# Start addresses of rings, pads, mask and unit matrix moved by 64 bytes in a kernel that mixes a Fourier layer with windowed attention

## The chip, the cores and the metric

One core of a Trainium2 chip. The metric is the device time of one execution in microseconds (us); below, "the time" is the median of three timed executions, and "the profiled execution" is one more, taken with the hardware profiler.

## The reference

The input `x` is 2048 rows of 512 floats. Two branches are computed from it and mixed row by row with a gate.

```
a = x @ dft_hid_re.T ; b = x @ dft_hid_im.T
A = dft_seq_re @ a - dft_seq_im @ b            # Fourier branch, 2048 x 512
q, k, v = split(x @ wqkv)                      # 32 heads of 16
s = q @ k.T / 4, masked to 0 <= i - j < 256    # window of 256 keys, causal
B = (softmax(s) @ v) @ wo                      # attention branch
g = sigmoid((x * gate_w).sum(-1))
out = g * A + (1 - g) * B
```

Everything is float32. The kernel splits each dense operand into a high part in the chip's `float32r` format and a low remainder, and adds three products (high by high, high by low, low by high).

## The kernel before

**Dense work.** `dense()` is a generator that yields after almost every matmul. It gives, in this order, the projections to queries and keys (line 281), to values and to the two Fourier intermediates (line 304), and then the big Fourier product (line 529). All are matmuls of a 128x128 weight tile with 512 moving columns. Their operands are the tiles `hi` and `lo` (weights or moving operand, split from `raw`) and the 16 buffers of `big`.

**Attention.** The 32 heads are done in 4 groups of 8, and each group in 32 blocks of 64 queries; one matmul does two heads of a block, so a block has four. The scores of a block against its window are computed twice, in two orientations. `s_pair` (line 367) takes a `pad0` tile as weights and up to 320 columns of `ring1` (keys) as moving operand; VectorE adds the `mask` and finds each row's extreme (line 369), ScalarE takes the exponential and its row sum (line 372). 19 blocks later `t_pair` (line 449) takes a `pad1` tile as weights and up to 320 columns of `ring0` (queries, and rows with the statistics) as moving operand; ScalarE writes the exponentials to a `pt` tile or, in the second half of the kernel, for two blocks in six, to a part of the tile `home` (line 450), GpSimd cuts two triangles out of it (lines 454 and 458), and `pv` (line 475) multiplies it with `vpad`. There are 512 matmuls of `s_pair` and 512 of `t_pair`; their moving operands begin at multiples of 64 columns, so of 256 bytes, behind the start of a ring. `make_pad` (lines 348 and 350) writes the pads from the rings, and `ring_load` fills the rings by DMA ahead of their use. `ident` is the moving operand of 32 small matmuls that turn the statistics (line 387).

**Order.** The main loop over the blocks calls `s_pair`, then `fill`, which takes a few steps of `dense()`, then `t_pair`, then `fill` again. So on TensorE one attention matmul is followed by two or so dense ones, all through the attention stage. The order on TensorE, VectorE, ScalarE and SyncE is that of the program.

**Tail.** When the attention is done, the rings hold something else: the output projection. It is done two blocks of rows at a time by seven products (a Strassen-like scheme) on TensorE at line 922, with 256 moving columns. `fin` names the places of the seven combinations of `wo` in the rings (moving operand), `spot`, `spots` and `os_spot` those of the combinations of the attention's output (weights). In the kernel before, all these places lie 16 floats (64 bytes) behind a multiple of 512 floats from the ring's start, and the last window of each ring row runs 16 floats into the next row; therefore `spots` has a second form that goes over the flat ring.

**Memory.** The pool `const` gives its tiles addresses in the order in which they are asked for, each behind the one before: the pads, `ring0`, `ring1`, `mask`, `ident`, `half` (a tile of 64 bytes with a few columns of scalars), `vpad`, `gl`, `g1`, `g0`, `home`, `ge`. The pools of the other tiles follow.

Of the kernel before, what the change touches and what calls it, by code (L numbers as in the profile page):

```python
# [7 lines left out]
F32 = mybir.dt.float32  # L8
# [6 lines left out]
P = 128  # L15
S = 2048
# [16 lines left out]
def fnet_window_mix(ctx: ExitStack, tc: tile.TileContext, xT, x, wqk, wv, wr, wi, cr, ci, wo, gw, out):  # L33
    nc = tc.nc

    const = ctx.enter_context(tc.tile_pool(name="const", bufs=1))
# [30 lines left out]
    @contextmanager  # L67
    def behind(*engines):
        with ExitStack() as es:
            for e in engines:  # L70
                if e in last:
                    es.enter_context(tc.issue_after(last[e]))
            yield
# [4 lines left out]
    def split(hi, lo, raw, act=False):  # L78
        if act:
            nc.scalar.copy(hi, raw)  # L80
        else:
            cast = (nc.gpsimd if act is None else nc.vector).tensor_copy(hi, raw)
            if act is None:
                mark("pool", cast)
        return nc.vector.tensor_sub(lo, raw, f(hi))
# [79 lines left out]


    NPAD = 2
    pads = [[const.tile([P, NP, P], F32R, name=f"pad{i}_{b}") for b in range(NPAD)] for i in range(2)]
    ring = [const.tile([P, NP, S], F32R, name=f"ring{i}") for i in range(2)]

# [2 lines left out]
    for h in (0, 64):  # L173
        m = mask[h:h + 64, :]
# [6 lines left out]
    mark("pool", nc.gpsimd.affine_select(ident[:], f(ident[:]), pattern=[[1, P]], compare_op=OP.is_equal, fill=0.0,  # L181
                                         base=0, channel_multiplier=-1))

    cols = const.tile([P, 16], F32, name="half")
    half, side = cols[:, :2], cols[:, 2:4]
    mrow = cols[:, 4:6]
    for h in range(2):
# [150 lines left out]
    def make_pad(i, n):  # L338
        if not 0 <= n < NG * NB:
            return  # L340
        t = pads[i][n % NPAD]
        b = n % NB
        with behind(*(("act", "dve") if n < NPAD else ("dve",) if i == 0 and n < 24 else ())):
            for h in range(2):
# [437 lines left out]
    def flat(i):  # L782
        return ring[i].rearrange("r p s -> r (p s)")

    def fin(m, h, c=None):
        at_c = m % 4 * S + 16 + 512 * h
        t = flat(m // 4)[:, at_c:at_c + 512].rearrange("p (c e) -> p c e", c=2)
        return t if c is None else t[:, c]

    def spot(i, p, c0):  # L790
        return flat(i)[:, p * S + c0:p * S + c0 + 512]

    def spots(i, n, c0):
        if c0 + 512 > S:
            return flat(i)[:, c0:c0 + n * S].rearrange("r (p s) -> r p s", s=S)[:, :, :512]
        return ring[i][:, :n, c0:c0 + 512]

    COL = 1040, 1552

    def os_spot(m, b):  # L800
        if m < 3:
            return spot(0, m, COL[b])
        if b and m == 6:
            return spot(0, 3, COL[0])
        return spot(1, m - 3, COL[b])

    def halves(t):
        return (t[:, :256], t[:, 256:]) if len(t.shape) == 2 else (t[:, :, :256], t[:, :, 256:])
# [22 lines left out]
    def fin_split(c, m):  # L831
        split(fin(m, 0, c), fin(m, 1, c), DIFF[c][m])
# [60 lines left out]
    def split_a(i):  # L893
        a, b = O[i][1]
        split(*halves(spots(0, 2, COL[i % 2])), a.rearrange("p (m t) -> p m t", m=2), True)
        split(*halves(os_spot(2, i % 2)), b[:, 256:], True)
# [4 lines left out]
    def wo_split(i):  # L901
        if i > 1:
            r_load(i)
        split_a(i)
        s = EX[i][:, :1024].rearrange("p (m t) -> p m t", m=4)
        n = 3 if i % 2 else 4
        split(*halves(spots(1, n, COL[i % 2])), s[:, :n], True)
        if i % 2:
            split(*halves(os_spot(6, 1)), s[:, 3], True)

    def wo_begin(i):
# [6 lines left out]
        def product(ps, m, n, start=True):  # L918
            o = os_spot(m, i % 2).rearrange("p (h c t) -> p h c t", h=2, c=2)
            for c in range(2):  # L920
                for a, b in TERMS:
                    nc.tensor.matmul(ps, o[:, a, c], fin(n, b, c), start=start and c == 0 and a + b == 0,  # L922
                                     stop=c == 1 and a == 1, skip_group_check=True)
# [189 lines left out]
```

## Time and profile before

| | |
|---|---|
| time, median of 3 | 846.09 us (845.69 to 846.45) |
| the profiled execution | 845.1 us, its span 843.3 us |
| TensorE (PE) busy | 838.5 us, 99% of the span |
| VectorE (DVE), ScalarE (ACT) busy | 643.8 us, 611.1 us |
| GpSimd (POOL) busy | 298.8 us |
| DMA | 161.03 MB, mean 191 GB/s |

The span is the time from the first to the last instruction that the profile shows. In the profile L367 is line 367 of the kernel; PE is TensorE's matmuls, PEld its weight loads, which run beside the matmul before. The durations of two matmuls in a row overlap (393 ns is the mean of line 529, which starts one about every 230 ns); what one costs in a full stream is read from the distance between starts, which the chain of waits shows: there each matmul has the time by which it held up the next.

### The profile page before, as it was taken

To read this page: it belongs to the slowest core of one execution; us is meant where nothing else is said; L and a number is where in the kernel's file an instruction comes from. 1 tells how busy PE (TensorE), PEld (TensorE's weight loads), DVE (VectorE), ACT (ScalarE), POOL (GpSimd) and SP (SyncE) were. 2 spreads that over 40 slices of the span, in tenths; PEclk is the share of its full clock that TensorE was granted. 3 is DMA by queue.
4 is the path that set the end of the run, shared out by engine and by line. 5 is a ranking of instruction groups with operands and counts; after the bars stand their busy time and mean duration, and the time that the engine had idled before them with its cause. 6 is when DMAs were issued, how large, how long until landed. Compare 5 with 4: busy or idle time off the path is not lost.

```text
span 843.3 us, 17171 instructions
## 1 busy us (share of the span) xinstructions
PE 838.5 (99%) x5310; PEld 695.8 (83%) x5310; DVE 643.8 (76%) x2083; ACT 611.1 (72%) x1832; POOL 298.8 (35%) x606
## 2 busy tenths in 40 slices
PE   9999999999999999999999999999999999999998
PEld 7888888888888888888888887878887878878997
DVE  5588978677979787787877877878987867666874
ACT  6488888878888897787877977867777865553430
POOL 8102333233232233342333243343242357756410
PEclk9999999999999999999999999999999999999999
DMA  8776678485766173534454547979874256455732
GB/s 295 251 227 187 217 243 283 159 259 202 220 222 189 54 232 107 177 120 121 140 160 126 168 153 223 298 214 309 274 216 149 96 179 198 137 192 196 220 133 92
DMA packets 94475, 161.03 MB, mean 191 GB/s; under 512 B 26800, under 2 KB 35504, under 8 KB 94384
## 3 DMA queue, kind: packets, MB, share of 16 engines
q1 hardware_dynamic: 93952, 159.28, 59.1%
q8 instruction: 42, 0.69, 0.3%
q10 hardware_dynamic: 432, 0.66, 0.2%
q14 instruction: 49, 0.40, 0.1%
HBM read 108.27 MB, written 51.64 MB: 190 GB/s over the span
## 4 chain that ended last, share of the span: by engine, by line
PE 99%; DVE 1%; issue 0%; ACT 0%; DVEq 0%; ACTq 0%
PE dc L529 42%; PE dab L304 11%; PE dqk L281 10%; PE t L449 9%; PE s L367 8%; PE o L475 8%; PE dv L304 5%; PE t L922 5%; PE s L269 1%; PE dv L593 0%; PE s L387 0%; DVE pad L350 0%; PE t L559 0%; DVE sm L369 0%; ACT sm L372 0%
## 5 line engine op out<-in xcount | busy, mean ns | idle before, releaser
L529 PE MATMUL dc<-big,hi 128*128 128x512 f32 x1020 | 344.7, 393 | 0.0
L369 DVE CUSTOM_DVE_ANT_0 sm<-s,mask 128x320 f32<-128x320 f32 (+4 forms) x512 | 235.5, 465 | 111.4 <-PE s L367 71.2
L372 ACT ACTIVATE sm<-sm,ml 128x320 f32<-128x320 f32 (+4 forms) x512 | 278.2, 544 | 56.4 <-DVE ml L369 52.1
L450 ACT ACTIVATE pt<-t 128x320 f32<-128x320 f32 (+4 forms) x392 | 159.5, 411 | 83.4 <-PE t L449 78.1
L529 PE MATMUL dc<-big,lo 128*128 128x512 f32 x510 | 200.2, 393 | 0.0
L529 PEld LDWEIGHTS dc<-big,hi 128*128 128x128 f32 x1020 | 179.3, 188 | 21.4
L454 POOL TENSOR_SCALAR_AFFINE_SELECT pt<-pt 128x128 f32<-128x128 f32 x196 | 77.1, 393 | 275.0 <-ACT pt L450 273.7
L449 PE MATMUL t<-ring,pad 128*128 128x320 f32 (+4 forms) x512 | 156.8, 306 | 0.0
L367 PE MATMUL s<-ring,pad 128*128 128x320 f32 (+4 forms) x512 | 154.9, 303 | 0.1
L350 DVE TENSOR_SCALAR pad<-ring,half 96x256 fp32r<-96x256 f32 x384 | 120.0, 359 | 5.4 <-PE t L449 4.9
L449 PEld LDWEIGHTS t<-ring,pad 128*128 128x128 f32 x512 | 96.1, 188 | 30.9 <-issue 8.7
L367 PEld LDWEIGHTS s<-ring,pad 128*128 128x128 f32 x512 | 96.2, 188 | 20.6 <-DVE ml L369 0.7
L529 PEld LDWEIGHTS dc<-big,lo 128*128 128x128 f32 x510 | 95.9, 188 | 12.0
L372 ACT ACTIVATION_READ_ACCUMULATOR sm<-sm,ml 128x1 f32 x512 | 98.1, 192 | 0.0
L588 DVE TENSOR_TENSOR lo<-raw,hi 128x512 fp32r<-128x512 f32 x137 | 94.3, 696 | 2.7 <-ACT hi L588 2.5
L304 PE MATMUL dab<-hi,big 128*128 128x512 f32 x256 | 88.9, 394 | 0.0
L281 PE MATMUL dqk<-big,hi 128*128 128x512 f32 x240 | 85.0, 393 | 0.0
L432 POOL TENSOR_SCALAR vpad<-vr,half 128x256 f32<-128x256 f32 x64 | 62.2, 983 | 62.1 <-PE o L475 29.5
L348 ACT ACTIVATE pad<-ring,half 96x256 fp32r<-96x256 f32 x128 | 66.9, 522 | 0.0
L454 POOL TENSOR_SCALAR_AFFINE_SELECT home<-home 128x128 f32<-128x128 f32 x60 | 33.8, 564 | 90.2 <-ACT home L450 85.7
L458 POOL TENSOR_SCALAR_AFFINE_SELECT pt<-pt 128x128 f32<-128x128 f32 x172 | 62.9, 366 | 0.0
L588 DVE CAST hi<-raw 128x512 fp32r<-128x512 f32 x126 | 54.3, 437 | 11.3 <-PE dc L529 10.6
(122 smaller groups left out, 1034.2 us busy)
## 6 DMA issues: line engine op xcount, KB each, us to landing
qk_scr<-home SPq DMA_DIRECT2D x32, 512.0 KB
ring<-qk_scr SPq DMA_DIRECT2D x32, 512.0 KB
raw<-cr SPq DMA_DIRECT2D x32, 512.0 KB
raw<-ci SPq DMA_DIRECT2D x32, 512.0 KB
r_scr<-ev SPq DMA_DIRECT2D x42, 256.0 KB
ab_scr<-home SPq DMA_DIRECT2D x20, 512.0 KB
big<-ab_scr SPq DMA_DIRECT2D x20, 512.0 KB
ring<-qk_scr SPq DMA_DIRECT2D x32, 256.0 KB
```

The costliest lines, as they stand in the source:

```text
L281: nc.tensor.matmul(ps, w[a][:, c:c + 128], XT[dk, ss][:, b], start=n == 0, stop=n == 11)
L304: nc.tensor.matmul(ps, XT[dk, ss][:, a, c * 128:(c + 1) * 128], wh[b], start=n == 0, stop=n == 11)
L350: mark(f"pad{i}", nc.vector.tensor_scalar(dst, src, half[:96, h:h + 1], None, op0=OP.mult))
L367: nc.tensor.matmul(ps[:, :w], PAD[0, n][:, p], ring[1][:, p, k0:k0 + w], start=True, stop=True)
L369: mark("dve", nc.vector.tensor_tensor_reduce(out=sm[:, :w], in0=ps[:, :w], in1=mask[:, WIN - w:], scale=1.0, scalar=3e38, op0=OP.add, op1= ...
L372: mark("act", nc.scalar.activation(sm[:, :w], sm[:, :w], AF.Exp, bias=nm[:, c], scale=-1.0, accum_out=l[:, c]))
L449: nc.tensor.matmul(ps[:, :w], PAD[1, n][:, p], ring[0][:, p, q0:q0 + w], start=True, stop=True)
L450: nc.scalar.activation(pt[:, p, :w], ps[:, :w], AF.Exp, scale=-1.0)
L454: nc.gpsimd.affine_select(a, a, pattern=[[0, 2], [2, 64]], compare_op=OP.is_ge, fill=0.0, base=1, channel_multiplier=-1)
L475: nc.tensor.matmul(OT[g, sb][32 * p:32 * p + 32, q - sb * 512:e - sb * 512], v2[:, p], pt[:, p, q - q0:e - q0], start=first, stop=kb == 8 ...
L529: nc.tensor.matmul(ps, w[a][:, i % 8 * 128:i % 8 * 128 + 128], ab[SC[i]][:, b], start=i == ends[0] and a + b == 0, stop=i == ends[1] and a ...
L588: return fn(*args)
```

## The change

The tile `half` of 64 bytes is asked for before the pads and no longer behind `ident`. So pads, rings, mask and unit matrix begin 64 bytes further on, and everything from `vpad` on stays where it was. In the tail, the places in the rings lose their offset of 16 floats, so that their addresses stay the same as before; the windows end at the ring row's end, and the second form of `spots` goes.

```diff
     NPAD = 2
+    cols = const.tile([P, 16], F32, name="half")
     pads = [[const.tile([P, NP, P], F32R, name=f"pad{i}_{b}") for b in range(NPAD)] for i in range(2)]
     ring = [const.tile([P, NP, S], F32R, name=f"ring{i}") for i in range(2)]
...
-    cols = const.tile([P, 16], F32, name="half")
     half, side = cols[:, :2], cols[:, 2:4]
...
     def fin(m, h, c=None):
-        at_c = m % 4 * S + 16 + 512 * h
+        at_c = m % 4 * S + 512 * h
...
     def spots(i, n, c0):
-        if c0 + 512 > S:
-            return flat(i)[:, c0:c0 + n * S].rearrange("r (p s) -> r p s", s=S)[:, :, :512]
         return ring[i][:, :n, c0:c0 + 512]

-    COL = 1040, 1552
+    COL = 1024, 1536
```

The start of the tiles within a partition, in bytes modulo 128, in the two programs:

| tile | before | after |
|---|---|---|
| pad0, pad1 (weights of lines 367 and 449) | 0 | 64 |
| ring0, ring1 (their moving operands) | 0 | 64 |
| mask (read by line 369), ident (moving operand of line 387) | 0 | 64 |
| output weights and attention's output in the rings (line 922) | 64 | 64 |
| half | 0 | 0 |
| home (moving operand of line 475 for part of the blocks) | 0 | 0 |
| vpad, big, hi, lo, raw, ev, pt, sm | 64 | 64 |

No instruction is added, removed or moved on any engine: the two programs have the same instructions in the same order, with the same shapes. One wait differs: a subtraction on VectorE that forms a low part of the output weights (line 85) waits for an instruction of ScalarE that lies five earlier than before.

## The prediction

> **What bounds the kernel now.** I read the busy times first, then the slices, then the chain of waits with its shares, then what TensorE waits for. The page of the kernel before opens so:
>
> ```profile
> span 843.3 us, 17171 instructions
> PE 838.5 (99%) x5310; PEld 695.8 (83%) x5310; DVE 643.8 (76%) x2083; ACT 611.1 (72%) x1832; POOL 298.8 (35%) x606
> PEclk9999999999999999999999999999999999999999
> ```
>
> ```profile
> core 0: 843.3 us, clock 1.000
> ```
>
> TensorE is busy all the time, and its granted clock is at 90% or more in every one of the 40 slices, 1.000 in the mean. That alone doesn't say that it bounds the kernel, since a waiting matmul can look busy; the chain of waits says it. Its shares by line:
>
> ```profile
> by line: PE dc L529 41.8%; PE dab L304 10.5%; PE dqk L281 9.5%; PE t L449 9.0%; PE s L367 8.4%; PE o L475 8.1%; PE dv L304 4.8%; PE t L922 4.8%; PE s L269 0.8%; PE dv L593 0.4%; issue 0.2%; PE s L387 0.2%; DVE pad L350 0.2%; PE t L559 0.2%;
> ```
>
> All but some tenths of a per cent are matmuls. Hence only what alters the distance between two matmuls can alter the time by much. The change touches 512 + 512 matmuls of lines 367 and 449: 17.4% of the span, 146.7 us. The question is whether those 146.7 us hold a cost of starting at 0 modulo 128, or whether starting at 64 brings one.
>
> **What a matmul costs at either start.** In the chain in order of time, a steady piece of the attention stage with both its operands at 0 (lines 367 and 449, 320 columns) between dense matmuls with both operands at 64 (line 529, 512 columns) reads (start, length in us):
>
> ```profile
> 496.53 0.15 PE s L367
> 496.68 0.45 PE dc L529 x2
> 497.13 0.15 PE t L449
> 497.28 0.45 PE dc L529 x2
> ...
> 501.93 0.15 PE t L449
> 502.08 0.45 PE dc L529 x2
> 502.53 0.15 PE s L367
> ```
>
> From 496.53 to 502.53 there are ten rounds of one attention matmul and two dense ones: 0.600 us a round, with no row that is late. Stages in which every operand begins at 64 show what those take alone, 512 columns in the projection to queries and keys, 256 in the output projection:
>
> ```profile
> 22.50 5.44 PE dqk L281 x24
> 765.42 2.87 PE t L922 x24
> ```
>
> 5.44 / 24 = 226.7 ns, and 2.87 / 24 = 119.6 ns. So two dense matmuls take 453.3 ns of the 600, and 146.7 ns are left for the attention matmul at 0. What would it take at 64? The two all-64 rows give a straight line: (226.7 - 119.6) / 256 = 0.418 ns a column, and 119.6 + 64 x 0.418 = 146.4 ns at 320 columns. **146.7 at 0 against 146.4 at 64**: 0.3 ns apart, less than the rounding of the rows (0.005 us in 2.87 is 0.2 ns).
>
> The Trainium skill, TensorE: Matmul & The Clock Gate, section "Back-to-back issue gap", has another rule: N / 2.4 + 2.5 ns from start to start at the full clock. That is 135.8 ns at 320 columns and 215.8 at 512; by it 1024 attention matmuls would be 1024 x 10.9 ns = 11.2 us cheaper than they are. The all-64 row above has 226.7 where the rule has 215.8, so a start at 64 doesn't give the rule's figure.
>
> The weight loads, which run beside the matmul before, have no better start either:
>
> ```profile
> L449 PEld LDWEIGHTS t<-ring,pad 128*128 128x128 f32 x512 | 96.1, 188 | 30.9 <-issue 8.7 <-DVE ml L369 0.8 <-DVE ev L496 0.5
> L529 PEld LDWEIGHTS dc<-big,hi 128*128 128x128 f32 x1020 | 179.3, 188 | 21.4
> ```
>
> 188 ns from a pad at 0, 188 ns from `hi` or `lo` at 64. And a matmul of line 475 reads its moving operand from `pt` at 64 or, in the second half, from `home` at 0:
>
> ```profile
> L475 PE MATMUL o<-pt,vpad 128*32 128x320 f32 x400 | 31.4, 436 | 0.0
> L475 PE MATMUL o<-home,vpad 128*32 128x320 f32 x112 | 9.6, 432 | 0.0
> ```
>
> 436 ns at 64 and 432 at 0; these are durations with waits in them, not distances, but if they say anything, 64 is the dearer.
>
> **The change part by part.**
>
> *Lines 367 and 449 with both operands at 64.* The trace shows no attention matmul at 64, so the cost lies between bounds. From above: 4 ns each, the difference of the two rows of line 475, 1024 x 4 = +4.1 us. From below: all that these lines take beyond the steady distance. For that I need their widths; per line there are 448 of 320 columns and 16 each of 256, 192, 128 and 64:
>
> ```profile
> L449 PE MATMUL t<-ring,pad 128*128 128x320 f32 x448 | 141.3, 316 | 0.0
> L367 PE MATMUL s<-ring,pad 128*128 128x320 f32 x448 | 139.6, 312 | 0.1
> L449 PE MATMUL t<-ring,pad 128*128 128x256 f32 x16 | 4.7, 294 | 0.0
> L367 PE MATMUL s<-ring,pad 128*128 128x64 f32 x16 | 3.1, 192 | 0.0
> ```
>
> 896 x 146.7 ns = 131.4 us, and by the straight line 32 x (119.6 + 92.8 + 66.1 + 39.3) ns = 10.2 us: 141.6 us of the 146.7. The other 5.1 us (the shares' rounding makes that 0.8 more or less) are waits and irregular steps, and if all of them came from the start at 0, the change would bring -5.1 us. I take the straight line, since its rows are the same kind of matmul in a full stream: 1024 x -0.3 ns = **-0.3 us**.
>
> *Line 922.* The places in the rings lose 16 floats where the rings gain 64 bytes: the same addresses as before, 0 us. The second form of `spots` named the same elements. *Line 387*: 32 matmuls with `ident` at 64, 0.2% of the span in all; 0.3 ns or 4 ns each is 0.1 us at most.
>
> *ScalarE, VectorE and GpSimd.* The mask is read, the pads written and the rings read from new starts. For ScalarE and VectorE the trace has the same operation with a tile at either start:
>
> ```profile
> L450 ACT ACTIVATE pt<-t 128x320 f32<-128x320 f32 x344 | 145.4, 427 | 68.2 <-PE t L449 63.3 <-PE s L367 3.9
> L450 ACT ACTIVATE home<-t 128x320 f32<-128x320 f32 x104 | 44.2, 425 | 7.0 <-PE t L449 5.9 <-POOL home L454 0.4
> L90 DVE TENSOR_TENSOR home<-dqk,home 128x512 fp32r<-128x512 f32 x15 | 10.2, 683 | 1.4 <-ACT home L88 1.4
> L90 DVE TENSOR_TENSOR big<-dab,big 128x512 fp32r<-128x512 f32 x12 | 8.2, 685 | 1.0 <-ACT big L88 1.0
> ```
>
> 427 at 64 and 425 at 0; 685 at 64 and 683 at 0. Two ns for each of the 512 operations of line 369, 512 of pads and some 100 of the tail are 2 us on engines that have over 190 us idle. What hides it is TensorE's own stream: what it waits for, with its weight loads, is this much:
>
> ```profile
> PE dv L593 <- DVE ev L151: 1.5, 1, 1.5
> PEld s L367 <- DVE ml L369: 0.7, 2, 0.5
> PEld t L449 <- DVE ml L369: 0.8, 3, 0.3
> ```
>
> The first is the start of the program, the two others are all of VectorE's statistics: 1.5 us. If that cover were gone, those 2 us would come on top. I take 0. For GpSimd the trace has no such pair at one time: it reads some tiles in the pads' places in the tail, off the chain, 0 as well.
>
> *The DMAs into the rings* have the same pieces and the same place in the queue; no row of TensorE waits for a DMA, so 0. *The one wait* that names an earlier instruction of ScalarE can only end earlier; VectorE is not late there, 0.
>
> **Sum:** 845.1 us of the profiled execution - 0.3 = 844.8. It lay 1.0 below the median of the three, 846.09, which is the number to be predicted: **845.8 us**, no change. A measurement of this kernel can tell about 0.2%, 1.7 us, from no change (the three lie 0.76 us apart).
>
> **The rivals.**
>
> *The start at 0 is behind the irregular steps: faster.* The 5.1 us would go in part or whole: 841.0 us with all of it. For it: the steps outside the steady rounds are there, and no row says that a start has no part in them. Against it: the rounds at 0 come at 0.600 us for long stretches, and a cost of the address would be there each time.
>
> *The fixed part of a matmul vanishes: faster still.* The line has 226.7 - 512 x 0.418 = 12.7 ns a matmul that don't depend on its columns. If they were paid for a pair of starts that disagree, and went where all agree, the attention matmuls would lose 1024 x 12.7 ns = 13.0 us: 833.1. Against it: the stages at 22.50 and 765.42 agree in all their starts and pay it. (The skill's rule of above would have 834.9.)
>
> *Streams that begin in the same place collide: slower.* In the attention stage the weights of the next matmul are now read beside a moving operand whose start differs by 64; after, all starts agree. If an attention matmul then costs 4 ns more, as the rows of line 475 would have it, it is +4.1 us, 850.2; with half of that 848.1. It decides from 1.7 us / 1024 = 1.7 ns on, a round of 0.6017. Against it: the all-64 stages lie on a line with the rounds.
>
> *The change doesn't do what it says:* `home` stays at 0, so a third of line 475's blocks in the second half keep their start. That costs nothing by the rows above, and the time would be the forecast's.
>
> **How the numbers follow.** No change (within 0.2%, 844.4 to 847.5): 0.60, the case without effect or with that of `home` left. Faster: 0.19 for the irregular steps, 0.05 for the fixed part, together 0.24. Slower: 0.16. The range goes from 840.5, just below the first rival's 841.0, to 849.5, between that of the slower one's half and whole; what is left out, the fixed part's 0.05 and the ends, is under 0.2. I doubt the middle most where the argument is weakest: both ends of the attention matmul are only extrapolated.
>
> **What would show it.** In the changed kernel's chain the rounds must again take 0.600 us, and lines 449 and 367 together 17.4% of the span; line 281's 24 matmuls 5.44 us and line 922's 2.87 us are untouched controls. Rounds of 0.597 or less, or shares that fall by 0.4, speak for the first rival; rounds of 0.602 or more for the slower one. If rounds and controls agree and the time still moves, the cause lies in waits on VectorE or ScalarE, and the rows of line 369 and 372 must show it. I would be wrong if the start mattered only together with something that a steady round hides, as a weight load that comes late.

## The result, and the profile after

The changed kernel takes **855.39 us** (855.27 to 856.44, 4 runs) against 846.00 (845.69 to 846.45, 4 runs) before: **slower, 1.0116 times** (95% interval 1.0104 to 1.0128). I forecast no change, 845.8, with a range up to 849.5. The page after, and the chain's shares by line:

```profile
span 853.5 us, 17171 instructions
PE 848.7 (99%) x5310; PEld 696.4 (82%) x5310; DVE 644.8 (76%) x2083; ACT 612.4 (72%) x1832; POOL 297.4 (35%) x606
by line: PE dc L529 42.1%; PE dab L304 10.7%; PE dqk L281 9.6%; PE t L449 8.8%; PE s L367 8.3%; PE o L475 8.0%; PE dv L304 4.8%; PE t L920 4.7%; PE s L269 0.7%; PE dv L593 0.4%; issue 0.2%; PE s L387 0.2%; DVE pad L350 0.2%; PE t L559 0.2%;
```

The span of the profiled execution grew by 10.2 us, the median time by 9.4. The other engines are busy hardly longer: VectorE 644.8 us for 643.8, ScalarE 612.4 for 611.1. The additions of the mask (line 369), which read it at 64 now, take 485 ns as before; the first row is of the kernel before, the second of the changed one:

```profile
L369 DVE CUSTOM_DVE_ANT_0 sm<-s,mask 128x320 f32<-128x320 f32 x448 | 215.4, 485 | 92.6 <-PE s L367 56.3 <-ACT sm L372 27.0 <-ACT home L88 1.9
L369 DVE CUSTOM_DVE_ANT_0 sm<-s,mask 128x320 f32<-128x320 f32 x448 | 215.5, 485 | 101.4 <-PE s L367 64.6 <-ACT sm L372 28.4 <-ACT home L88 2.1
```

The shares hide where the time is. Lines 367 and 449, whose operands moved, have 17.1% of 853.5 us, 145.9, a little less than before; the dense lines, whose operands did not move, have more. So the views to read are those that go by place. Three pieces of the chain that stand at the same point of both programs, before:

```profile
323.08 3.39 PE o L475 x80
726.79 3.39 PE o L475 x80
765.42 2.87 PE t L922 x24
```

and after (start and length in us):

```profile
22.43 5.44 PE dqk L281 x24
327.20 3.39 PE o L475 x80
736.77 3.39 PE o L475 x80
775.58 2.87 PE t L920 x24
```

The delay is 4.1 us at 323, 10.0 at 727 and 10.2 at 765, and no more from there to the end. It accrues through the whole stage in which attention and dense matmuls take turns. The two controls that I named, 24 dense matmuls in 5.44 us and 24 of the output projection in 2.87, are what they were. And this is the attention stage at the same place as in the prediction:

```profile
498.40 0.15 PE s L367
498.55 0.47 PE dc L529 x2
499.02 0.15 PE t L449
499.17 0.47 PE dc L529 x2
...
504.60 0.15 PE s L367
```

From 498.40 to 504.60 there are ten rounds: **0.620 us a round, where it was 0.600**. The dense pair takes 0.47 instead of 0.45, and the attention matmul some 2 ns more. Nothing waits: every piece is a matmul. In other stretches of the changed kernel a round takes 0.607, ten of them from 405.01 to 411.08:

```profile
405.01 0.14 PE t L449
405.16 0.46 PE dc L529 x2
...
411.08 0.14 PE t L449
```

These rounds account for the loss. The two programs have the same matmuls in the same order, so their starts can be compared one by one: the 640 rounds of one 320-column attention matmul and two dense ones take 8.4 us longer in all, 13 ns each; the 113 rounds with three dense ones bring 0.6 us, and everything between 1.2.

### The profile page after: what moved, and what is told of

It reads as the page before. It is cut to its first block, busy times and chain, and to the rows that moved or that the text cites. A ratio compares the mean times of both kernels' runs of the same rounds, so it can differ in the third digit from the quotient of the medians.

```text
span 853.5 us, 17171 instructions
## 1 busy us (share of the span) xinstructions
PE 848.7 (99%) x5310; PEld 696.4 (82%) x5310; DVE 644.8 (76%) x2083; ACT 612.4 (72%) x1832; POOL 297.4 (35%) x606
## 4 chain that ended last, share of the span: by engine, by line
PE 99%; DVE 1%; issue 0%; ACT 0%; DVEq 0%; ACTq 0%
PE dc L529 42%; PE dab L304 11%; PE dqk L281 10%; PE t L449 9%; PE s L367 8%; PE o L475 8%; PE dv L304 5%; PE t L920 5%; PE s L269 1%; PE dv L593 0%; PE s L387 0%; DVE pad L350 0%; PE t L559 0%; DVE sm L369 0%; ACT sm L372 0%
## 5 line engine op out<-in xcount | busy, mean ns | idle before, releaser
L529 PE MATMUL dc<-big,hi 128*128 128x512 f32 x1020 | 348.7, 397 | 0.0
L454 POOL TENSOR_SCALAR_AFFINE_SELECT home<-home 128x128 f32<-128x128 f32 x60 | 32.0, 535 | 92.9 <-ACT home L450 83.2
```

The source lines that it names most:

```text
L454: nc.gpsimd.affine_select(a, a, pattern=[[0, 2], [2, 64]], compare_op=OP.is_ge, fill=0.0, base=1, channel_multiplier=-1)
L529: nc.tensor.matmul(ps, w[a][:, i % 8 * 128:i % 8 * 128 + 128], ab[SC[i]][:, b], start=i == ends[0] and a + b == 0, stop=i == ends[1] and a ...
```

## The experiments

I tested these theories. A: TensorE reads two streams at once, the moving operand of one matmul and the weights of the next, and what counts is the distance between their starts; in its first form modulo 128, later modulo 256. B: 64 itself is a bad start for the attention's operands, its pads or its rings. C: it is the mask at 64, read by VectorE. E: other engines or DMAs in the same memory take part.

The variants differ in addresses alone, except for the two with matmuls only. The table has the distance from the dense tiles' start to that of pads and rings modulo 256, worked out from the order and the sizes of the tiles, and what each took; the ratio is to the kernel before on the same chip. Four variants (e7, e8, e10, e11) also set `dynamic_dma_scratch_size` of the program to 512 in place of 1024; e11, which has it, takes the time of the kernel before. Several of the variants move `vpad` too, or the dense tiles against it; where 80 matmuls of line 475 stand together, they take 3.39 us in every whole kernel.

| run | pads, rings: start modulo 128 | dense: start modulo 128 | distance modulo 256 | time | ratio to before (95%) |
|---|---|---|---|---|---|
| before | 0 | 64 | 192 | 846.0 | |
| changed | 64 | 64 | 0 | 855.39 | 1.0116 (1.0104 to 1.0128) |
| e1_mirror | 64 | 0 | 64 | 851.00 | 1.0059 (1.0043 to 1.0076) |
| e2_all0 | 0 | 0 | 0 | 855.08 | 1.0109 (1.0094 to 1.0124) |
| e3_pads64 | pads 64, rings 0 | 64 | pads 0, rings 64 | 855.26 | 1.0111 (1.0096 to 1.0126) |
| e4_rings64 | pads 0, rings 64 | 64 | pads 192, rings 0 | 850.76 | 1.0059 (1.0044 to 1.0074) |
| e5_shift128 | 0 | 64 | 64 | 851.54 | 1.0073 (1.0058 to 1.0088) |
| e6_by32 | 32 | 64 | 224 | 850.83 | 1.0064 (1.0049 to 1.0079) |
| e7_st0 | 0 | big 64, hi and lo 0 | 192 to big, 128 to hi and lo | 848.03 | 1.0031 (1.0020 to 1.0042) |
| e8_all_differ | pads 0, rings 64 | big 64, hi and lo 0 | pads to big 192, rings to hi and lo 192 | 852.50 | 1.0087 (1.0071 to 1.0104) |
| e10_dist128 | 64 | 64 | 128 | 847.48 | 1.0031 (1.0019 to 1.0042) |
| e11_restored | 64 | 0 | 192 | 845.44 | 1.0000 (0.9990 to 1.0010) |

**e1_mirror** and **e2_all0: which side moved?** The scratch tile `ge` goes, so that all pools behind `const` begin 64 bytes earlier. e1 does it to the changed kernel, e2 to the kernel before.

```diff
-            e = const.tile([P, 16], F32, name="ge")
+            e = g0
```

> Rings, pads, mask and unit matrix begin at 64 as in the changed kernel, and every tile of the dense work (big, hi, lo, raw, ev, pt, sm) begins at 0 instead of 64 modulo 128. Theory A (it costs when a matmul's weights and the moving operand that streams beside their load begin at the same place modulo 128): attention and dense differ again, so rounds of 0.600 us as in the kernel before, and its time, 846 within 2. Theory B (64 itself is the bad start for the attention's operands): rounds of 0.607 to 0.620, 855. Theory C (it is the mask that VectorE reads at 64): 855.

> The kernel before with the tiles of the dense work at 0 modulo 128 as well, so that all operands of the attention's rounds begin at 0 and none at 64. Theory A (same start): as slow as the changed kernel, rounds of 0.607 to 0.620, 855 within 2. Theory B (64 is bad for the attention's operands): rounds of 0.600, 846. Theory C (mask at 64): 846.

e2 takes 855.08 with the attention's operands at 0 and none at 64: B in the form of a bad start at 64 falls, and so does C, since its mask is at 0. What e2 and the changed kernel share is that all starts agree, and e2 has the same rounds of 0.620 and 0.607. But e1, where they differ by 64 modulo 128 as before the change, takes 851.0, half-way, and A modulo 128 had said 846. Its rounds:

```profile
496.21 0.14 PE s L367
496.35 0.47 PE dc L529 x2
496.82 0.14 PE t L449
496.96 0.46 PE dc L529 x2
497.42 0.14 PE s L367
```

0.61 and 0.60 in turn, here and in most of the stage: the same two addresses modulo 128 in exchanged roles are not the same.

**e3_pads64** and **e4_rings64: one part of the change alone.** The 64-byte tiles are asked for in another order.

```diff
+    cols = const.tile([P, 16], F32, name="half")     # e3: ahead of the pads
     pads = ...
+    gl = const.tile([P, 16], F32, name="gl")         # e3: rings stay at 0; e4: cols here instead
     ring = ...
```

> Pads alone at 64, rings, mask and unit matrix at 0 as before. Theory A (same start): the pads' load now agrees with the dense operand that streams beside it, the load of the dense weights still differs from the ring that streams; two overlaps of a round agree in place of one before and three in the changed kernel, so between 848 and 853, rounds of about 0.607. Theory B in the form that the ring's start counts: 846; in the form that the pads' start counts: 855. Theory C: 846.

> Rings, mask and unit matrix at 64, pads at 0. Theory A (same start): the load of the dense weights now agrees with the ring that streams beside it, the pads' load differs from the dense operand; two of three overlaps agree, between 848 and 853. Theory B in the form that the ring's start counts: 855; in the form that the pads' start counts: 846. Theory C (mask at 64): 855.

Either alone is slower, pads by as much as the whole change and rings by half. A had both between 848 and 853, so e3 missed it. B in its pads' form had e3 right but 846 for e4, in its rings' form 846 for e3 and 855 for e4, and e2 speaks against both. e3 is not clean: it also moves rings, mask, unit matrix and `vpad` by 128 bytes, a thing that only counts if the distance isn't taken modulo 128. C had 855 for e4 and 846 for e3: wrong again.

**e5_shift128** asks that question alone: `half` and `gl` before the pads move pads, rings, mask and unit matrix by 128 bytes, so that every start modulo 128 is that of the kernel before (`vpad` moves by 128 as well). **e6_by32** moves them by 32, with an offset of 8 floats for the places of the output projection in the rings.

```diff
+    cols = const.tile([P, 16], F32, name="half")     # e6: [P, 8], without gl
+    gl = const.tile([P, 16], F32, name="gl")
     pads = ...
```

> Pads, rings, mask and unit matrix 128 bytes further on than before, so the same modulo 128 (0, dense at 64) and no longer the same modulo 256: attention minus dense is +64 where the kernel before has -64. Theory A128 (what counts is the distance of two operands' starts modulo 128): as the kernel before, 846 within 1.5, steady rounds of 0.600 us. Theory A256 (the distance counts modulo 256, so the mirror run differed from the kernel before because its distance was +64): as the mirror run, 851, rounds that alternate between 0.600 and 0.613.

> Pads, rings, mask and unit matrix 32 bytes further on than before, half of the change; the output weights keep their addresses by an offset of 8 floats. If lines of 64 bytes count (the start lies in the same line as before): 846, rounds of 0.600. If the distance counts byte by byte: between, 848 to 853. If a start in the middle of a line costs a fetch more for each operand: above 855.

e5 takes 851.54 where a theory modulo 128 needs 846, and its rounds alternate between 0.61 and 0.60 like the mirror's, which has the same distance of +64:

```profile
497.21 0.15 PE t L449
497.36 0.46 PE dc L529 x2
497.82 0.15 PE s L367
497.96 0.46 PE dc L529 x2
498.42 0.14 PE t L449
```

So it is not the distance modulo 128 that counts; A takes it **modulo 256** from here on, and e12 shows below that a distance of 256 does what 0 does. e6 is between, 850.83: a start within the same 64 bytes isn't the same start.

**e7_st0** and **e8_all_differ: the dense operands among themselves.** A spare tile of 64 bytes ahead of `hi` and `lo` moves them and the pools behind, `big` stays.

```diff
+    st.tile([P, 16], F32, bufs=1, name="gap")        # e8: with the rings of e4
```

> The kernel before with hi, lo and the tiles behind them 64 bytes further on, at 0 modulo 128, big still at 64: dense weights and the dense moving operand now differ, while the ring (0) and the dense weights (0) that load beside it agree. Theory A (what agrees costs): one overlap of three agrees in a round of line 529, as before: 846 to 851, and the dense stage alone, where all agreed before, may fall under 5.44 us for 24 matmuls. Theory D (a dense matmul's 13 ns over its columns are fixed): 5.44 us again.

> Pads at 0, rings at 64, hi and lo at 0, big at 64: in line 529 every load of weights differs by 64 from the moving operand that streams beside it. Theory A: no slow rounds at all, at or under the kernel before, 842 to 846. Theory B in the form that the ring's start counts by itself: as the run with the rings alone at 64, 851.

Both are slower than the kernel before, 848.03 and 852.50; "what agrees costs" in its plain form falls with e8, where nothing agrees in the rounds of line 529 and they take 0.607 all the same. e7's loss lies elsewhere: it is 2.4 us behind at the 80 matmuls of line 475 that begin at 323.08 in the kernel before, and 2.5 us at the output projection, so the later rounds with line 529 cost it next to nothing. The dense stage alone shows that agreement can be the best. e7 (its lines stand one further down):

```profile
23.00 5.60 PE dqk L282 x24
```

5.60 / 24 = 233.3 ns a matmul, where both kernels have 226.7 with all starts equal. It is not a fixed cost either: the distance counts for dense matmuls too, with its best elsewhere.

**e10_dist128: all starts at 64, and not slow.** The changed kernel's starts modulo 128, with spare tiles that make the distance 128 modulo 256.

```diff
+    const.tile([P, 32], F32, name="front")
     cols = const.tile([P, 16], F32, name="half")
...
+    const.tile([P, 96], F32, name="gap")             # ahead of vpad, whose start modulo 256 stays
```

> Pads, rings, mask and unit matrix 128 bytes (modulo 256) from the dense tiles, 64 modulo 128 as in the changed kernel, dense untouched. Theory A128 (the distance modulo 128): as the changed kernel, 855, steady rounds of 0.607 or 0.620. Theory A256: its own pattern, not that of the changed kernel; between 846 and 855.

847.48: every TensorE operand that the change names begins at 64 modulo 128, exactly as in the changed kernel, but only 2.3 us are left of its 9.4 (845.18 is the kernel before on this chip).

**e11_restored: undo the change from the other side.** The changed kernel, with the dense tiles moved on as well.

```diff
     home = const.tile([P, 3072], F32R, name="home")
+    const.tile([P, 16], F32, name="spare")
```

> The changed kernel with the dense tiles (big, hi, lo, raw, ev, pt, sm) moved on as well, to 0 modulo 256, so that the attention's operands, at 192 modulo 256, are again 192 bytes past a dense start, as before the change. Modulo 128 every start is that of the mirror run (attention 64, dense 0), which took 851. Theory A256 (the distance modulo 256 counts): as the kernel before, 846 within 1.5, long stretches of rounds of 0.600 us. Theory A128 or any theory of single starts modulo 128: as the mirror run, 851, rounds that alternate between 0.600 and 0.613.

845.44, the kernel before in time (ratio 1.0000, 0.9990 to 1.0010), with the mirror's starts modulo 128:

```profile
496.25 0.15 PE t L450
496.39 0.45 PE dc L530 x2
496.85 0.15 PE s L368
497.00 0.45 PE dc L530 x2
497.45 0.15 PE t L450
```

**e9_micro** and **e12_distances: the matmuls alone.** One tile of zeros, matmuls only, places d bytes apart. e9 has all matmuls on one line, which the chain runs together, so its times below are differences of starts in its trace; e12 has a line for each role.

From e12, cut to its rounds:

```python
def rounds(d, per):          # d in floats here
    for i in range(24):
        w, m = PAD + i % 4 * 128 + d, RING + i % 4 * 512 + d
        nc.tensor.matmul(ps[1][:, :320], a[:, w:w + 128], a[:, m:m + 320], start=True, stop=True)
        for j in range(per):
            w, m = W + j % 2 * 128, M + (2 * i + j) % 4 * 512
            nc.tensor.matmul(ps[0], a[:, w:w + 128], a[:, m:m + 512], start=True, stop=True)
```

> Only matmuls on one tile of zeros, no other engine at work, no part of the reference's computation: 24 dense matmuls (512 columns) with weights d bytes off the moving operand's place modulo 512, the same for 320 columns, then 24 rounds of one 320-column matmul (its weights and its moving operand both d off) and two dense ones, then the same with only its weights, and with only its moving operand off. Theory A256 (two streams that TensorE reads at once, weights and moving operand, get in each other's way by their distance modulo 256): the whole kernel's effect is here without VectorE, ScalarE, DMA: rounds of 0.600 us at d = 192, of 0.607 or 0.620 at d = 0, alternating 0.600 and 0.613 or steady 0.613 at d = 64, the same again at d + 256; dense alone 226.7 ns at 0 and 233.3 at 64. Theory E (it needs other engines or DMAs that read or write the same memory): rounds of 0.600 at every d.

> Matmuls alone once more, nothing of the reference's computation, each role on a line of its own: 24 dense matmuls with weights d bytes off the moving operand, d = 0 to 256 in steps of 32; then 24 rounds of one 320-column matmul, both its operands d off, and two, one or three dense ones whose operands agree; each set entered once after 8 matmuls of 512 columns and once after 8 of 256. Theory A256: dense alone 5.44 us at 0 and at 256, 5.5 to 5.6 between; 24 rounds with two dense 14.40 at 192, 14.48 at 128, 14.57 at 64, and at 0 and 256 14.56 or 14.85 by the way of entry; with one dense and with three the same order, 192 at the floor of 24 x 0.373 = 8.96 and 24 x 0.827 = 19.84, and 0 above it. Rival (the order belongs to rounds of two dense alone): with one or three dense ones another distance than 192 is the best, or 0 as good.

e9 is busy on TensorE for 803.6 of 813.7 us, with VectorE's one fill of the tile, four small constants on GpSimd and one DMA of the tile as the only other work of the program, all over at 22 us, before the first set of rounds at 170. It shows the effect at full size, 14.40 us for 24 rounds at 192 and 14.56 or 14.85 at 0 and 256, so E falls. Two more things it shows. 24 matmuls of 320 columns by themselves take 3.51 to 3.53 us at every distance, 146.4 to 147.3 ns each. And both operands count: with the weights of the 320-column matmul alone 192 off, as in e4, 24 rounds take 14.57, with its moving operand alone 64 off, as in e3, 14.74, and none of the sixteen sets with one operand moved comes to 14.40. e12's dense matmuls alone, 24 a row, at d = 0, 64, 192 and 256:

```profile
15.06 5.44 PE ps L31 x24
...
29.73 5.60 PE ps L31 x24
...
59.51 5.49 PE ps L31 x24
...
74.25 5.44 PE ps L31 x24
```

and the 8 matmuls that stand between the sets of 24 rounds with two dense ones, d = 0 to 256 in steps of 32; a set begins where the 8 before end (start + length), and ends where the next 8 start:

```profile
79.69 1.81 PE ps L36 x8
96.06 1.82 PE ps L36 x8
112.54 1.81 PE ps L36 x8
128.92 1.85 PE ps L36 x8
145.45 1.84 PE ps L36 x8
161.77 1.85 PE ps L36 x8
178.33 1.81 PE ps L36 x8
194.54 1.82 PE ps L36 x8
210.92 1.83 PE ps L36 x8
227.32 1.81 PE ps L36 x8
```

| d, bytes | 0 | 32 | 64 | 96 | 128 | 160 | 192 | 224 | 256 |
|---|---|---|---|---|---|---|---|---|---|
| 24 rounds, us | 14.56 | 14.66 | 14.57 | 14.68 | 14.48 | 14.71 | **14.40** | 14.56 | 14.57 |

For instance 194.54 - (178.33 + 1.81) = 14.40 at 192, 0.600 a round: the kernel before is at the best of the nine. The whole kernels follow this order: 128 (e10) 847.5 us, 64 and 224 (e1, e5, e6) 850.8 to 851.5; at 0 the changed kernel's rounds of 0.620 make it slower still. 0 costs 0.16 more in 24 rounds, 0.607 a round, which is one of the two values of the changed kernel. The other one comes at the same distance by another way in. Entered after 8 matmuls of 256 columns in place of 512, the set at d = 256 takes 14.86 us in place of 14.57, while that at 192 again takes the least, 14.41. The set at 256 reads at its end

```profile
366.38 0.15 PE ps L41
366.53 0.47 PE ps L44 x2
367.00 0.15 PE ps L41
367.15 0.47 PE ps L44 x2
367.62 0.15 PE ps L41
```

0.620 a round, the changed kernel's rows. So the distance sets which rounds can repeat, and what ran just before picks one of them.

The rival of e12 has a point. With one dense matmul to an attention one, 24 rounds took 9.04 us at 192 (expected was the floor, 8.96) and 8.96 at 224; with three they took 19.84 at 192 after 512 columns and 20.31 after 256. (These are differences of starts in its trace, like those above.) The best distance belongs to the rhythm; 192 is that of two dense ones, which most of this kernel's rounds have.

No version beat the kernel before; e11 equals it.

## Why the prediction was wrong, point by point

*What bounds the kernel* was right: TensorE's stream, and only the distance between matmuls could move the time. That the other engines, the DMAs, the output projection and the one changed wait would cost nothing was right as far as the runs show: the rows of line 369 and the 2.87 us of the output projection are unchanged, and the effect is there in e9 and e12 without any of them.

**The step that failed** is the term "Lines 367 and 449 with both operands at 64": I took a matmul's cost as its own, a straight line through two stages in which every operand begins at 64, and put 146.4 ns at 320 columns against 146.7 measured at 0. -0.3 us came out; 10.2 us of span was measured, 10.0 ns for each of 1024 attention matmuls. Both rows of the line were right and did not bear on the question. In each of those stages one kind of matmul follows itself, and such a stream runs at its floor when all starts agree: 5.44 in e12, and in e9 the 146.5 ns of 320 columns that the line had foretold. In a round the kinds alternate, and there the same agreement costs 7 or 20 ns (0.607 or 0.620). The stage alone was no model of the mixture.

*My bound from above* failed with it. The 4 ns of `pt` against `home` came from durations, and from a matmul beside others of its kind again. A bound that includes the neighbours would have had to come from a row where attention and dense matmuls alternate at another distance, and the trace before has none: pads and rings lie 192 bytes past the dense starts in all of it. What it did have is rounds other than 0.600, the 5.1 us that I put down to waits and irregular steps; I didn't ask why rounds without a wait were ever longer. The prediction's last sentence, that the start might matter only together with a weight load that a steady round hides, came nearest, and it had no price in the sum.

*The rivals.* "Streams that begin in the same place collide" named the streams that theory A names and had the right side, with 0.16. I dismissed it by the all-64 stages, the same mistake once more, and gave it 4 ns for 10. That its side came out is in part luck, since the plain mechanism was too simple: by e8 and by e12 it is not agreement that costs but the distance modulo 256, and 64, 96 or 160 can be as bad as 0 or worse. "The start at 0 is behind the irregular steps" falls with e11, where no pad and no ring begins at 0 and nothing is gained. "The fixed part of a matmul vanishes" falls with the change itself, where all starts agree, and with e12, where no stream of 512 columns comes under 226.7 ns. "`home` stays at 0" had no part: every operand of line 475 keeps its start, and its 80 matmuls take 3.39 us in both kernels. A slip in the numbers: 844.4, the lower end of "no change", is 1.7 below 846.09, while the upper end is 1.7 above 845.8; around the forecast it would be 844.1.

*The signs that I set:* rounds of 0.620 spoke for the slower rival, and the two controls of 5.44 and 2.87 stood still. The share of lines 367 and 449 would have misled: I had put a fall of 0.4 down to the faster rival, and it fell from 17.4% to 17.1% in a slower kernel, because the chain gives the lost time of a mixed round mostly to the dense matmuls.

What stays open is the circuit. That the place of the weights against the moving operand counts is shown by the dense matmuls alone, where nothing else differs. Which pair counts in the mixed rounds is not shown: the next weights and the operand that streams beside their load are theory A's reading, but whenever such a distance changed there, one between successive weights or between successive moving operands changed with it. Nor is it shown why 192 is good. Many rounds lie in steps of 6.7 ns (0.600, 0.607, 0.613, 0.620), but not all: in e10 they alternate between 0.598 and 0.608, in e3 they repeat 0.607, 0.610 and 0.623.

## What to carry to other kernels

An alignment is not a property of one tile. Where weights stream in beside a moving operand, the distance between their starts modulo 256 was worth 1.1% of this TensorE-bound kernel, and the good distance belongs to the rhythm of the stream: measure it with a loop of matmuls alone in that rhythm, as e12 does, and keep it when a small tile is added or reordered ahead of large ones.

A stage with one kind of matmul was no evidence here for a mixture, however exact its rows were. And when time is lost without a wait, look at the length of a round in the chain, not at the shares by line.

## What the runs showed of the hardware that I had not expected

- The time of a stream of matmuls depends on how far apart weights and moving operands begin, modulo 256 bytes: 24 rounds of the same matmuls take 14.40 us at 192, 14.56 at 0, 14.71 at 160; e1 and e5 (64 by different addresses) have the same alternating rounds, and e11 the 0.600 of the kernel before. The Trainium skill, TensorE: Matmul & The Clock Gate, section "Step-by-step: what each phase is for", holds that loading the next tile's weights doesn't steal read bandwidth from the running matmul. In these float32r streams the place of the weights alone takes 24 dense matmuls from 5.44 to 5.60 us; that doesn't fit the sentence, and the measurement decides.
- The rounds lock. At one and the same distance, 256, a stream repeats at 0.607 or at 0.620 us (14.57 and 14.86 us for 24 rounds in e12), by what ran just before it.
- Dense matmuls alone cost 226.7 ns when both operands' starts agree modulo 256 and 233.3 at 64 (5.44 and 5.60 us for 24), in e7's kernel as in the loop alone.
